# Attention and feed-forward kernel: the products with v moved from two steps of a pair into all five

## The chip, the cores and the metric

One NeuronCore of a Trainium2 chip. The metric is the device time of one execution in microseconds (us).

## The reference

```python
scores = q @ k.T / sqrt(D) + bias[h]        # per batch b, head h; bias from a small MLP on log distances
attn = exp(scores - max) / (sum + 1e-9)
out = attn @ v                              # B=4, H=8, S=576, D=64
x = out, heads side by side                 # 2304 x 512
h = x @ w_in                                # 512 x 2048
y = (h * tanh(softplus(h))) @ w_out         # 2304 x 512
```

All in float32.

## The kernel before

The program has three stages. The first makes the bias of all heads and writes it to DRAM (`make_h`, `mirrored`, `evac`). The second is attention, the loop over `step(n)`. The third is the feed-forward part in blocks of 512 or 256 tokens (`hidden`, `gate`, `project`).

The schedule is written by hand: each engine takes its instructions in the order in which the code calls them.

Attention goes by pairs: pair i is two heads of one batch, 16 pairs in all. The 576 query rows of a pair are cut into five chunks c: four of 128 rows for each of the two heads, and one (c = 4) with the last 64 rows of both heads in one tile. A pair has five steps, x = 0 to 4, that take the chunks in `ORDER = [0, 1, 4, 2, 3]`. So step x = 2 is the short one. What a step n does:

- `scores(n)` (L218) on TensorE: three passes of q @ k.T with high and low parts (L227), into one or two PSUM tiles `s` of a pool of two.
- `add_bias(n)` (L230) on VectorE: one instruction a head, adds the bias and finds the row extreme (L241). It frees the tile `s`.
- `exps` (L246) on ScalarE: exponentials with row sums (L256).
- `transposes(n - 2)` (L304): the chunk of two steps before is turned on TensorE in blocks of 128 keys (L296), and ScalarE copies the blocks into `main` (L313, L316). `main` and `tail` belong to a group: group 0 of a pair is chunks 0 and 1 (256 queries), group 1 is chunks 4, 2 and 3 (320 queries).
- `turn_tails` (L318), at x = 2 and x = 4: the last 64 keys of both heads of several chunks, and at x = 2 the reciprocals of the row sums (L325, L333, L337, L338), copied by ScalarE (L343).
- `products` (L345): o = v.T @ turned probabilities for one group, five blocks k of keys (the fifth is `tail`) for two heads, accumulated in one PSUM tile `o` of a pool of one (L352).
- `collect` (L355): VectorE copies `o` to `x` (L360), SP stores `x` to `x_d` (L362, L364, L365).
- `ahead` (L397): loads for later pairs: q and k (`load_hi` on POOL's queue, `load_raw` on SP's), `load_v`, and in every fourth pair the bias of the next heads.
- `split` (L422): VectorE makes the low part of the next pair's q and k, and converts a piece of the weights of the third stage (float64 to float32 by shifts and masks).

In the steady state `products(i - 1, 1)` stands at x = 2 before the transposes and `products(i, 0)` at x = 4 after them, each followed by its `collect` at the end of the same step.

Of the kernel before, what the change touches and what calls it, by code (L numbers as in the profile page):

```python
# [7 lines left out]
F32 = mybir.dt.float32  # L8
# [11 lines left out]
P = 128  # L20
# [24 lines left out]
def kernel(ctx: ExitStack, tc, qk, v, wb, w2, w_in, w_out, psia, psi4, rinv, eye, out):  # L45
    nc = tc.nc
    pe, dve, act, pool, sp = nc.tensor, nc.vector, nc.scalar, nc.gpsimd, nc.sync
# [46 lines left out]
    def load_weights():  # L94
        while todo and len(w64) < 2:
            kind, g, k = job = todo.pop(0)
            w = convp.tile([P, 512, 2], U32, name="w64")
            if kind == "i":
                src = w_in[k * P:(k + 1) * P, g * 512:(g + 1) * 512]
            else:  # L100
                src = w_out[(4 * g + k) * P:(4 * g + k + 1) * P, :]
            sp.dma_start(out=w.rearrange("p f t -> p (f t)"), in_=src.bitcast(U32))
            w64.append((job, w))
# [66 lines left out]
    def load_raw(i):  # L170
        hp, b = divmod(i, B)
        raw = rawp.tile([P, QW], F32, name="rawqk")
        if i < 2:
            dve.memset(raw[:, 0:1], 0.0)
        sp.dma_start(out=raw, in_=qk[b, hp])
        qk_raw[i] = raw

    def load_v(i):
        hp, b = divmod(i, B)
        vt = vp.tile([P, 2, 5, D], F32, name="vt")  # L180
        sp.dma_start(out=vt, in_=v[b, hp].rearrange("p (h c d) -> p h c d", h=2, c=5))
        v_t[i] = vt

    def load_hi(i):
        hp, b = divmod(i, B)
        hi = hip.tile([P, QW], F32R, name="qkhi", bufs=3)
        pool.dma_start(out=hi, in_=qk[b, hp])
        qk_hi[i] = hi
# [7 lines left out]
    def load_bias(hp, c):  # L196
        h0, h1 = 2 * hp, 2 * hp + 1
        rows = P if c < 4 else 64
        src = bias_d[c][:, :rows * PITCH].rearrange("h (i j) -> h i j", j=PITCH)[:, :, PAD:PAD + S]
        t = bias_t[hp, c] = biasp.tile([P, 2 * S if c < 4 else 640], F32, name=f"bias{c}")[:, :2 * S if c < 4 else S]  # L200
        if c < 4:
            sp.dma_start(out=t[:, 0:S], in_=src[h0])
            sp.dma_start(out=t[:, S + 64:], in_=src[h1, :, 0:512])
            sp.dma_start(out=t[:, S:S + 64], in_=src[h1, :, 512:S])
        else:
            for r in range(2):
                sp.dma_start(out=t[r * 64:r * 64 + 64], in_=src[h0 + r])

    NPAIR = B * HP
    steps = [(i, c) for i in range(NPAIR) for c in ORDER]  # L210
    steps[4:7] = [(1, ORDER[0]), (1, ORDER[1]), (0, ORDER[4])]
    NS = len(steps)
    pt_t, live, o_t, sums, rc = {}, {}, {}, {}, {}
# [16 lines left out]
    def add_bias(n):  # L230

        i, c = steps[n]
        bt = bias_t[i // B, c]
        m = st.tile([P, 2], F32, name="m")
        if c < 4:
            pt = pp.tile([P, 2 * S], F32, name="pt")
        else:
            pt = p4p.tile([P, 640], F32, name="pt4")[:, :S]
        for u, s in enumerate(live[n]):
            sl = slice(u * S, (u + 1) * S)  # L240
            dve.tensor_tensor_reduce(  # L241
                out=halves(pt[:, sl]), in0=s[:, :, :SH], in1=halves(bt[:, sl]),
                scale=-0.125, scalar=BIG, op0=ALU.add, op1=ALU.min, accum_out=m[:, u:u + 1])
        live[n] = (pt, m)

    def exps(n, u):  # L246

        i, c = steps[n]
        if u == 1 and c == 4:
            return  # L250
        if i not in sums:
            sums[i] = st.tile([P, 9], F32, name="sums", bufs=3)
        pt, m = live[n]
        ps = pt[:, u * S:(u + 1) * S]
        k = 4 * u + c if c < 4 else 8
        act.activation(ps, ps, AF.Exp, bias=m[:, u:u + 1], scale=-1.0, accum_out=sums[i][:, k:k + 1])  # L256
# [5 lines left out]
        dve.reciprocal(r, r)  # L262
        return r

    turned, pts = [], {}

    def store_reciprocals():
        i, turned_r = turned.pop()
# [17 lines left out]
    def x_tile():  # L286
        return xs.tile([P, 320], F32, name="x", bufs=2)
# [54 lines left out]
        for tail, off, c, w, rows in copies:  # L342
            act.copy(tail[rows, off:off + w], tp[rows, c:c + w])  # L343

    def products(i, grp):  # L345
        main, tail = pt_t.pop((i, grp))
        vt = v_t[i]
        w = 256 if grp == 0 else 320
        o_t[i, grp] = o = o_ps.tile([P, 512], F32, name="o")
        for k in range(5):  # L350
            for h in range(2):
                pe.matmul(o[h * 64:h * 64 + 64, :w], vt[:, h, k, :], main[:, h, k, :] if k < 4 else tail,  # L352
                          start=(k == 0), stop=(k == 4), skip_group_check=True)

    def collect():  # L355
        (i, grp), o = o_t.popitem()
        hp, b = divmod(i, B)
        w = 256 if grp == 0 else 320
        x = x_first.pop() if x_first else x_tile()
        dve.tensor_copy(x[:, :w], o[:, :w])  # L360
        if grp == 0:
            sp.dma_start(out=x_d[b][:, hp, 0:256], in_=x[:, :256])  # L362
        else:
            sp.dma_start(out=x_d[b][:, hp, 256:512], in_=x[:, 64:320])  # L364
            sp.dma_start(out=x_d[b][:, hp, 512:576], in_=x[:, 0:64])  # L365
# [7 lines left out]
    def load_x(blk, p):  # L373
        t0, n = blocks[blk]
        raw = p.tile([P, HP, TB], F32, name="xraw", bufs=1)
        for off, m, b, s in _x_runs(t0, n):
            sp.dma_start(out=raw[:, :, off:off + m], in_=x_d[b][:, :, s:s + m])
        x_raw[blk] = raw

    def load_r(blk, r, h0, h1):  # L380

        t0, n = blocks[blk]
        for off, m, b, s in _x_runs(t0, n):
            while m:
                k = min(m, 512 - s) if s < 512 else m
                for u in range(2):
                    if s < 512:
                        src = r_d[b][h0:h1, 4 * u:4 * u + 4].rearrange("p c j -> p (c j)")[:, s:s + k]
                    else:
                        src = r_d[b][h0:h1, 8, 64 * u + s - 512:64 * u + s - 512 + k]  # L390
                    sp.dma_start(out=r[64 * u:64 * u + 64, :, off:off + k],
                                 in_=src.unsqueeze(0).to_broadcast([64, h1 - h0, k]))
                off, m, s = off + k, m - k, s + k
# [3 lines left out]
    def ahead(n):  # L397

        i, x = divmod(n, 5)
        if n == 4:  # L400
            pool.tensor_copy(gate_t, live[n][1][:, 0:1])
        if x == (1 if i else 4) and i + 2 < NPAIR:
            load_hi(i + 2)
            load_raw(i + 2)
        if (n == 9 or x == 3 and i > 1) and i + 1 < NPAIR:
            load_v(i + 1)
        if n == 5:
            load_weights()
        if i % B == B - 1 and i // B + 1 < HP:
            load_bias(i // B + 1, ORDER[x])  # L410
        if n == NS - 11:
            load_x(0, x0)
        if n in (NS - 10, NS - 6):
            x_r[0] = x0.tile([P, 2, TB], F32, name="xr", bufs=1)
            h0 = 0 if n == NS - 10 else 2
            load_r(0, x_r[0], h0, h0 + 2)
        if n in (NS - 7, NS - 3):
            h0 = 0 if n == NS - 7 else 2
            for d in range(2):
                pool.tensor_tensor(x_raw[0][:, h0 + d], x_raw[0][:, h0 + d], x_r[0][:, d], op=ALU.mult)  # L420
# [14 lines left out]
    def step(n):  # L435
        i, x = divmod(n, 5)
        back = n - LAG

        def exponentials():
            if n < NS:  # L440
                exps(n, 0)
                exps(n, 1)

        if n < NS:
            scores(n)
            add_bias(n)
        if n == 9:
            products(0, 1)
        elif x == 2 and n > 7:
            turn_tails((i - 1, 2), (i - 1, 3))  # L450
            products(i - 1, 1)
            exponentials()
        for k in (0, 1) if n == 3 else (back,):
            if k < NS:
                transposes(k)
        if n == 5:
            turn_tails((0, 2))
        elif n == 8:
            turn_tails((0, 3), (1, 0), (1, 1))
        elif n == 9:  # L460
            turn_tails((1, 4))
        elif x == 4:
            turn_tails((i, 0), (i, 1), (i, 4))
        if x != 2 or n == 7:
            exponentials()
        if x == 4 and n != 9:
            products(i, 0)
        elif n == 8:
            products(1, 0)
        if n < NS:  # L470
            ahead(n)
        if n <= NS and steps[n - 1][1] == ORDER[4]:
            rc[steps[n - 1][0]] = reciprocals(steps[n - 1][0])
        if n < NS:
            split(n)
        if turned:
            store_reciprocals()
        if o_t:
            collect()


# [40 lines left out]
    for idx in range(NB + 2):  # L522
# [4 lines left out]
        if idx + 2 < NB:  # L527
            n = reach(ts[idx + 2])[2]
# [79 lines left out]
    o_ps = lpsum("o_ps", 1)  # L608
# [248 lines left out]
```

## Time and profile before

| | |
|---|---|
| median of 3 runs | 715.35 us (714.86 to 715.86) |
| the profiled execution | 714.97 us |
| its span, first to last instruction | 713.0 us |
| TensorE busy (PE) | 670.4 us, 94% |
| VectorE busy (DVE) | 518.3 us, 73% |
| ScalarE busy (ACT) | 461.2 us, 65% |

PE is TensorE's matmuls, PEld its weight loads, DVE VectorE, ACT ScalarE, POOL GpSimd, SP SyncE. Idle time before an instruction is put down to what released it. Matmul rows overlap, because they are pipelined; where the argument needs what one costs, it goes by the starts of neighbouring rows. In the trace a float32 matmul of the products is two instructions, so x20 there is ten matmuls.

### The profile page before, as it was taken

How to read it: one execution, taken by the hardware profiler on the slowest of the kernel's cores; microseconds unless marked ns; L12 is line 12 of the kernel's file. 1: busy time of each engine (PE TensorE's matmuls, PEld its weight loads, DVE VectorE, ACT ScalarE, POOL GpSimd, SP SyncE). 2: the span in 40 equal slices, each digit the busy share in tenths (PEclk: the TensorE clock that was granted, in tenths of full speed). 3: DMA queues.
4: the chain of work that ended last, by engine and by line, in shares of the span. 5: the costliest groups of instructions: out<-in, count | busy, mean ns of one | idle time of the engine just before them, and what ended most of it. 6: DMA issues, size and time to landing. Idle time of an engine off the chain costs nothing.

```text
span 713.0 us, 14055 instructions
## 1 busy us (share of the span) xinstructions
PE 670.4 (94%) x5456; PEld 520.2 (73%) x5456; DVE 518.3 (73%) x1053; ACT 461.2 (65%) x949; POOL 17.9 (3%) x27
## 2 busy tenths in 40 slices
PE   6988989988999898898999999999999999999997
PEld 3546666666667666666878888889988888888886
DVE  7896677777887777558888888875675666665564
ACT  6987788878888888745565656553645454444443
POOL 0000000000000002100000000000000000000000
PEclk9999999999999999999999999999999999999999
DMA  8888677558647755050123312304141000010001
GB/s 278 271 272 288 225 236 248 171 171 282 196 169 222 255 177 155 27 158 29 60 88 105 103 59 60 112 7 119 60 112 36 1 1 0 1 59 1 1 0 60
DMA packets 46435, 86.94 MB, mean 122 GB/s; under 512 B 13200, under 2 KB 22048, under 8 KB 46368
## 3 DMA queue, kind: packets, MB, share of 16 engines
q1 hardware_dynamic: 43488, 75.32, 33.5%
q0 software_dynamic: 2304, 10.49, 4.6%
q8 instruction: 43, 0.70, 0.4%
q10 hardware_dynamic: 576, 0.22, 0.1%
q14 instruction: 24, 0.20, 0.1%
HBM read 64.56 MB, written 21.45 MB: 121 GB/s over the span
## 4 chain that ended last, share of the span: by engine, by line
PE 76%; DVE 14%; ACT 4%; DMA 2%; issue 2%; SPq 1%; DVEq 0%; ACTq 0%
PE y L702 24%; PE h L657 24%; PE o L352 11%; PE s L227 9%; DVE pt L241 6%; PE bps L557 5%; PE tp L296 2%; PE tp L325 1%; DVE e L680 1%; DVE e L664 1%; DVE w L134 1%; ACT bt L563 1%; DVE e L679 1%; DMA bias<-bias_d 1%; DVE w L127 1%
## 5 line engine op out<-in xcount | busy, mean ns | idle before, releaser
L241 DVE CUSTOM_DVE_ANT_0 pt<-s,bias 128x576 f32<-128x576 f32 x144 | 103.8, 754 | 38.0 <-PE s L227 35.1
L702 PE MATMUL y<-who,ghi 128*128 128x512 f32 x288 | 112.5, 391 | 2.5 <-ACT ghi L681 1.6
L702 PE MATMUL y<-who,glo 128*128 128x512 f32 x288 | 112.4, 390 | 1.3 <-DVE glo L684 1.3
L681 ACT CAST ghi<-e 128x512 fp32r<-128x512 f32 x72 | 44.7, 621 | 105.5 <-DVE e L680 99.4
L256 ACT ACTIVATE pt<-pt,m 128x576 f32<-128x576 f32 x144 | 111.5, 782 | 1.5 <-DVE m L241 1.1
L702 PE MATMUL y<-wlo,ghi 128*128 128x512 f32 x288 | 112.2, 390 | 0.0
L313 ACT COPY main<-tp 128x512 f32<-128x512 f32 x126 | 67.9, 592 | 37.3 <-PE tp L296 36.5
L657 PE MATMUL h<-xhi,whi 128*128 128x512 f32 (+1 forms) x320 | 80.0, 372 | 1.7 <-ACT xhi L632 1.7
L684 DVE TENSOR_TENSOR glo<-e,ghi 128x512 fp32r<-128x512 f32 x72 | 49.7, 691 | 42.0 <-ACT ghi L681 42.0
L657 PE MATMUL h<-xhi,wli 128*128 128x512 f32 (+1 forms) x320 | 79.5, 371 | 0.0
L657 PE MATMUL h<-xlo,whi 128*128 128x512 f32 (+1 forms) x320 | 78.8, 368 | 0.0
L227 PE MATMUL s<-qkhi 64*128 64x288 f32 (+1 forms) x288 | 54.4, 353 | 22.3 <-DVE m L241 22.2
L662 ACT ACTIVATE e<-h 128x512 f32<-128x512 f32 x72 | 42.7, 593 | 45.7 <-PE h L657 45.7
L663 DVE TENSOR_SCALAR e<-e 128x512 f32<-128x512 f32 x72 | 30.6, 425 | 55.7 <-ACT e L662 55.7
L352 PE MATMUL o<-main,vt 128*64 128x320 f32 (+1 forms) x512 | 69.1, 412 | 0.9 <-ACT main L313 0.9
L657 PEld LDWEIGHTS h<-xhi,whi 128*128 128x128 f32 x320 | 57.6, 189 | 13.5 <-ACT xhi L632 2.6
L657 PEld LDWEIGHTS h<-xhi,wli 128*128 128x128 f32 x320 | 57.5, 190 | 10.1
L702 PEld LDWEIGHTS y<-who,ghi 128*128 128x128 f32 x288 | 54.1, 188 | 14.5 <-ACT ghi L681 2.5
L657 PEld LDWEIGHTS h<-xlo,whi 128*128 128x128 f32 x320 | 57.1, 189 | 10.1
L702 PEld LDWEIGHTS y<-who,glo 128*128 128x128 f32 x288 | 54.1, 188 | 14.2 <-DVE glo L684 2.9
L702 PEld LDWEIGHTS y<-wlo,ghi 128*128 128x128 f32 x288 | 54.1, 188 | 10.8
L227 PEld LDWEIGHTS s<-qkhi 64*128 64x128 f32 (+1 forms) x288 | 29.6, 186 | 41.4 <-DVE m L241 35.0
(71 smaller groups left out, 1048.6 us busy)
## 6 DMA issues: line engine op xcount, KB each, us to landing
bias_d<-bt SPq DMA_DIRECT2D x36, 295.5 KB
qkhi<-in_qk_dram POOLq DMA_DIRECT2D x16, 640.0 KB, 4.7
rawqk<-in_qk_dram SPq DMA_DIRECT2D x16, 640.0 KB
w<-in_w_in_dram SPq DMA_DIRECT2D x16, 512.0 KB
w<-in_w_out_dram SPq DMA_DIRECT2D x16, 512.0 KB
vt<-in_v_dram SPq DMA_DIRECT2D x16, 320.0 KB
bias<-bias_d SPq DMA_DIRECT2D x16, 288.0 KB
out_dram<-w SPq DMA_DIRECT2D x17, 256.0 KB
```

Of the source, the lines that this page charges most:

```text
L227: pe.matmul(live[n][h][:, j, :SH], stat[rows, c * P:(c + 1) * P], mov[rows, k0:k0 + SH], start=(k == 0), stop=(k == 2))
L241: dve.tensor_tensor_reduce(out=halves(pt[:, sl]), in0=s[:, :, :SH], in1=halves(bt[:, sl]), scale=-0.125, scalar=BIG, op0=ALU.add, op1=ALU. ...
L256: act.activation(ps, ps, AF.Exp, bias=m[:, u:u + 1], scale=-1.0, accum_out=sums[i][:, k:k + 1])
L313: (dve.tensor_copy if n < 2 and u else act.copy)(blocks[:, :, off + 64 * u:off + 64 * u + 64], tp)
L352: pe.matmul(o[h * 64:h * 64 + 64, :w], vt[:, h, k, :], main[:, h, k, :] if k < 4 else tail, start=(k == 0), stop=(k == 4), skip_group_chec ...
L557: pe.matmul(ps[cg * 32:cg * 32 + 32, a:b], w2t, src, start=True, stop=True)
L657: pe.matmul(h[:, u * n:(u + 1) * n], w["i", g4, d][:, r * P:(r + 1) * P], x[:, d, :n], start=(k == 0), stop=(k == 11))
L662: act.activation(e, h, AF.Exp)
L663: dve.tensor_scalar(e, e, E20, None, op0=ALU.min)
L681: act.copy(ghi, e)
L684: dve.tensor_tensor(glo, e, ghi.bitcast(F32), op=ALU.subtract)
L702: pe.matmul(ys[blk][t], g[:, c0:c0 + P], w, start=((blk, f) in first and k == 0), stop=((blk, f) in last and k == 2))
```

## The change

`products` takes a range of blocks k, and from the third pair on (n > 11) the ten matmuls of a group are called in several steps. Group 1 of the pair before: blocks 0 and 1 at x = 2, blocks 2 to 4 at x = 3. Group 0: block 0 at x = 4, blocks 1 and 2 at x = 0 of the next pair, 3 and 4 at x = 1. `collect` follows the step with block 4. `load_v` moves from x = 3 to x = 4, since v of the pair before is now read at x = 3. The calls of `turn_tails` are the same ones as before. The last blocks of the last pair follow in `step(80)` to `step(82)`.

```diff
--- before.py
+++ after.py
@@ -262,7 +262,7 @@
         dve.reciprocal(r, r)
         return r
 
-    turned, pts = [], {}
+    turned, done, pts = [], [], {}
 
     def store_reciprocals():
         i, turned_r = turned.pop()
@@ -342,18 +342,23 @@
         for tail, off, c, w, rows in copies:
             act.copy(tail[rows, off:off + w], tp[rows, c:c + w])
 
-    def products(i, grp):
-        main, tail = pt_t.pop((i, grp))
+    def products(i, grp, ks=range(5)):
+        main, tail = pt_t[i, grp]
         vt = v_t[i]
         w = 256 if grp == 0 else 320
-        o_t[i, grp] = o = o_ps.tile([P, 512], F32, name="o")
-        for k in range(5):
+        if 0 in ks:
+            o_t[0] = o_ps.tile([P, 512], F32, name="o")
+        for k in ks:
             for h in range(2):
-                pe.matmul(o[h * 64:h * 64 + 64, :w], vt[:, h, k, :], main[:, h, k, :] if k < 4 else tail,
+                pe.matmul(o_t[0][h * 64:h * 64 + 64, :w], vt[:, h, k, :], main[:, h, k, :] if k < 4 else tail,
                           start=(k == 0), stop=(k == 4), skip_group_check=True)
+        if 4 in ks:
+            del pt_t[i, grp]
+            done.append((i, grp))
 
     def collect():
-        (i, grp), o = o_t.popitem()
+        i, grp = done.pop()
+        o = o_t[0]
         hp, b = divmod(i, B)
         w = 256 if grp == 0 else 320
         x = x_first.pop() if x_first else x_tile()
@@ -402,7 +407,7 @@
         if x == (1 if i else 4) and i + 2 < NPAIR:
             load_hi(i + 2)
             load_raw(i + 2)
-        if (n == 9 or x == 3 and i > 1) and i + 1 < NPAIR:
+        if x == 4 and 0 < i < NPAIR - 1:
             load_v(i + 1)
         if n == 5:
             load_weights()
@@ -448,7 +453,7 @@
             products(0, 1)
         elif x == 2 and n > 7:
             turn_tails((i - 1, 2), (i - 1, 3))
-            products(i - 1, 1)
+            products(i - 1, 1, range(2 if n < NS else 5))
             exponentials()
         for k in (0, 1) if n == 3 else (back,):
             if k < NS:
@@ -463,10 +468,13 @@
             turn_tails((i, 0), (i, 1), (i, 4))
         if x != 2 or n == 7:
             exponentials()
-        if x == 4 and n != 9:
-            products(i, 0)
-        elif n == 8:
-            products(1, 0)
+        if n in (4, 8):
+            products(n // 8, 0)
+        elif n > 11:
+            if x == 3:
+                products(i - 1, 1, range(2, 5))
+            elif x != 2:
+                products(i if x == 4 else i - 1, 0, {4: (0,), 0: (1, 2), 1: (3, 4)}[x])
         if n < NS:
             ahead(n)
         if n <= NS and steps[n - 1][1] == ORDER[4]:
@@ -475,7 +483,7 @@
             split(n)
         if turned:
             store_reciprocals()
-        if o_t:
+        if done:
             collect()
```

TensorE in the steady state, from the tails of x = 2 to the transposes of x = 3, before (s are scores, tp blocks being turned, o products with v):

```order
L325 MATMUL tp<-ident,pt 128x128 x2
L333 MATMUL tp<-ident,sums 9x128
L352 MATMUL o<-main_3555,vt 64x320 x8
L352 MATMUL o<-tail_3556,vt 64x320 x2
L296 MATMUL tp<-ident,pt 128x64 x16
L227 MATMUL s<-qkhi 128x288 x4
L227 MATMUL s<-qklo,qkhi 128x288 x4
L227 MATMUL s<-qkhi,qklo 128x288 x4
L296 MATMUL tp<-ident,pt 128x64 x16
```

The same steps in the changed kernel:

```order
L325 MATMUL tp<-ident,pt 128x128 x2
L333 MATMUL tp<-ident,sums 9x128
L353 MATMUL o<-main_3812,vt 64x320 x4
L296 MATMUL tp<-ident,pt 128x64 x16
L227 MATMUL s<-qkhi 128x288 x4
L227 MATMUL s<-qklo,qkhi 128x288 x4
L227 MATMUL s<-qkhi,qklo 128x288 x4
L296 MATMUL tp<-ident,pt 128x64 x16
L353 MATMUL o<-main_3812,vt 64x320 x4
L353 MATMUL o<-tail_3813,vt 64x320 x2
```

The products of 320 columns, one run of ten matmuls before, are two pieces now: four before the transposes of x = 2, and six after those of x = 3.

TensorE from the tails of x = 4 on, before:

```order
L325 MATMUL tp<-ident,pt 128x128 x2
L337 MATMUL tp<-ident,pt_3697 64x128
L338 MATMUL tp<-ident,pt_3697 128x128
L352 MATMUL o<-main_3716,vt 64x256 x8
L352 MATMUL o<-tail_3717,vt 64x256 x2
L227 MATMUL s<-qkhi 128x288 x4
L227 MATMUL s<-qklo,qkhi 128x288 x4
L227 MATMUL s<-qkhi,qklo 128x288 x4
L296 MATMUL tp<-ident,pt 128x64 x16
L227 MATMUL s<-qkhi 128x288 x4
```

The same places in the changed kernel, up to the last products of the group in x = 1:

```order
L353 MATMUL o<-main_3710,vt 64x256 x2
L227 MATMUL s<-qkhi 128x288 x4
L227 MATMUL s<-qklo,qkhi 128x288 x4
L227 MATMUL s<-qkhi,qklo 128x288 x4
L296 MATMUL tp<-ident,pt 128x64 x16
L353 MATMUL o<-main_3710,vt 64x256 x4
L227 MATMUL s<-qkhi 128x288 x4
L227 MATMUL s<-qklo,qkhi 128x288 x4
L227 MATMUL s<-qkhi,qklo 128x288 x4
L296 MATMUL tp<-ident,pt 128x64 x16
L353 MATMUL o<-main_3710,vt 64x256 x2
L353 MATMUL o<-tail_3711,vt 64x256 x2
```

The products of 256 columns were ten matmuls in a row; now two stand after the tails, four after the transposes of x = 0 and four after those of x = 1.

VectorE from the end of x = 2 on, before (ISA is the bias add and the read of its result):

```order
L120 TENSOR_SCALAR low<-w_3851 128x512
L271 COPY rt<-tp 9x128
L360 COPY x<-o 128x320
L241 ISA pt,m<-s,bias_4063 128x576
L241 ISA m 128x1
L241 ISA pt,m<-s,bias_4063 128x576
L241 ISA m 128x1
L127 SCALAR_TENSOR_TENSOR w_4331<-high,low 128x512
```

And in the changed kernel:

```order
L120 TENSOR_SCALAR low<-w_3843 128x512
L271 COPY rt<-tp 9x128
L241 ISA pt,m<-s,bias_4057 128x576
L241 ISA m 128x1
L241 ISA pt,m<-s,bias_4057 128x576
L241 ISA m 128x1
L127 SCALAR_TENSOR_TENSOR w_4325<-high,low 128x512
L365 COPY x<-o 128x320
```

The copy x<-o of the group of 320 columns has moved from the end of x = 2 to the end of x = 3, behind two bias adds and a conversion.

## Rows read from the trace of the kernel before

**Rows 1.** Busy by stretch: length, PE, PEld, DVE, ACT, POOL; clock, DMA share, GB/s

```profile
84.80:290.89 206.09, 186.54 (x2251) 137.12 (x2253) 159.68 (x387) 173.04 (x438) 12.09 (x15) 1.00 0.64 202
```

**Rows 2.** Timeline of PE (start, us, ...): such products, first and 14th

```profile
84.80 1.57 PE L352 MATMUL o<-main,vt 128*64 128x320 f32 x10 [0.20 <-ACT main L313]
...
290.83 2.37 PE L352 MATMUL o<-main,vt 128*64 128x320 f32 x16
```

**Rows 3.** Waits, 84.80 to 290.89 us: us in total, times, longest

```profile
ACT main L313 <- PE tp L296: 32.6, 33, 1.7
...
DVE pt L241 <- PE s L227: 25.2, 38, 1.0
PE s L227 <- DVE m L241: 19.2, 65, 0.4
...
PEld tp L296 <- issue: 6.4, 13, 0.5
```

**Rows 4.** Timeline of PE in one pair, from x = 2

```profile
178.18 0.53 PE L227 MATMUL s<-qkhi 128*128 128x288 f32 x2 [0.24 <-DVE m L241]
...
179.08 0.38 PE L325 MATMUL tp<-ident,pt 128*128 128x128 f32 x2
...
179.52 2.37 PE L352 MATMUL o<-main,vt 128*64 128x320 f32 x16
...
182.36 0.71 PE L296 MATMUL tp<-ident,pt 64*128 64x64 f32 x16
182.89 0.51 PE L227 MATMUL s<-qkhi 64*128 64x288 f32 x4
...
183.77 0.75 PE L296 MATMUL tp<-ident,pt 64*128 64x64 f32 x16
...
186.23 0.54 PE L296 MATMUL tp<-ident,pt 64*128 64x64 f32 x8
186.69 0.44 PE L325 MATMUL tp<-ident,pt 128*128 128x128 f32 x2
186.97 0.27 PE L337 MATMUL tp<-ident,pt 128*64 128x128 f32 x1
187.08 0.27 PE L338 MATMUL tp<-ident,pt 128*128 128x128 f32 x1
187.28 1.95 PE L352 MATMUL o<-main,vt 128*64 128x256 f32 x16
189.06 0.60 PE L352 MATMUL o<-tail,vt 128*64 128x256 f32 x4
189.59 0.54 PE L227 MATMUL s<-qkhi 64*128 64x288 f32 x4
...
190.49 0.66 PE L296 MATMUL tp<-ident,pt 64*128 64x64 f32 x16
```

**Rows 5.** Timeline of DVE in the same pair

```profile
182.48 0.49 DVE L360 COPY x<-o 128x320 f32<-128x320 f32 x1
183.96 0.76 DVE L241 CUSTOM_DVE_ANT_0 pt<-s,bias 128x576 f32<-128x576 f32 x1 [0.99 <-PE s L227]
...
186.43 0.76 DVE L241 CUSTOM_DVE_ANT_0 pt<-s,bias 128x576 f32<-128x576 f32 x1 [0.42 <-PE s L227]
...
190.69 0.76 DVE L241 CUSTOM_DVE_ANT_0 pt<-s,bias 128x576 f32<-128x576 f32 x1 [0.56 <-PE s L227]
...
193.27 0.75 DVE L241 CUSTOM_DVE_ANT_0 pt<-s,bias 128x576 f32<-128x576 f32 x1
```

**Rows 6.** Timeline of ACT in the same pair

```profile
183.17 0.59 ACT L313 COPY main<-tp 128x512 f32<-128x512 f32 x1 [1.16 <-PE tp L296]
```

**Rows 7.** Busy in a pair that loads bias, columns as rows 1

```profile
227.00:242.77 15.77, 14.35 (x176) 10.54 (x175) 11.96 (x30) 13.54 (x36) 0.53 (x1) 1.00 0.94 307
```

**Rows 8.** Timeline where attention meets the third stage

```profile
301.64 1.07 ACT L313 COPY main<-tp 128x512 f32<-128x512 f32 x2 [0.48 <-PE tp L296]
...
303.28 1.31 PE L657 MATMUL h<-xhi,whi 128*128 128x512 f32 x2 [1.68 <-ACT xhi L632]
```

## The prediction

> **What bounds the kernel now.** I read the busy times by stage first, then the waits of the middle stage, then TensorE's timeline through one pair, then VectorE's through the same pair.
>
> The change touches only the attention loop. From 84.80 us to 290.89 us there are 13 repetitions of one pair: the products of a second group start at 84.80 us, and 13 pairs later at 290.83 [rows 2], 206.03 / 13 = 15.85 us each. No engine fills it: ScalarE is busy 173.04 / 13 = 13.31 us of a pair, VectorE 12.28, TensorE 14.35 by its busy rows [rows 1]. In the waits [rows 3] three engines wait for one another: ScalarE's copies of turned blocks for the transposes (32.6 us, 2.5 a pair), VectorE's bias adds for the scores, the scores for the bias adds.
>
> The timeline says why [rows 4]. Of the five steps of a pair (x = 0 to 4) two carry all products: x = 2 from 179.52 to 182.36, x = 4 from 187.28 to 189.59. In those TensorE is late and VectorE waits 0.99 and 0.56 us for scores [rows 5]. In the other three TensorE has scores and transposes only, some 1.4 us, and is held by the two score buffers: scores may start when the bias adds of the step before have read theirs. That loop, bias add to bias add, takes 186.43 - 183.96 = 2.47 us [rows 5]. So a pair is two steps bound by TensorE and three by the loop.
>
> **TensorE's own work in a pair**, from start to start of neighbouring rows [rows 4], since busy rows overlap. Scores: 0.90 (x = 2), 0.88 (x = 3), 0.90 (x = 0); 0.89 taken for x = 1 and 4, whose rows hold waits; 4.46 in all. Transposes: 0.53 for 16 (182.36 to 182.89), four times, and 0.46 for x = 4: 2.58. Tails: 0.44 (179.08 to 179.52) and 0.59 (186.69 to 187.28): 1.03. Products: 2.84 + 2.31 = 5.15. Sum 13.22; so 15.85 - 13.22 = 2.63 us a pair are waits.
>
> The Trainium skill (Perfetto Trace Analysis, Identifying the Most-Contended Engine) says that matmul busy time is no good measure of TensorE's headroom, because the instructions are pipelined. Here by the busy rows there would be 15.85 - 14.35 = 1.50 us a pair to win, less 0.54 for the new edges below: 13 x 0.96 = 12.5 us, an end at 702.5 us. The starts give more room and bear the page out.
>
> **What the change adds and moves.**
> - *Products.* Nothing is removed; ten matmuls of each group stay, but one block k (two matmuls) goes to x = 4, two to x = 0, two to x = 1 (256 columns, 1.78 / 8 = 0.22 us a matmul), and for 320 columns two blocks to x = 2 and three to x = 3 (0.275 us a matmul, (2.84 - 0.09) / 10).
> - *New edges.* Products use other shapes of the array (128*64) than their neighbours (64*128, 128*128). Two groups become five, so three more entries and three more exits. In the rows an exit costs 189.59 - 189.06 - 2 x 0.22 = 0.09 us, and an entry 187.28 - 187.08 = 0.20 against 0.11 between the transposes before it, again 0.09. Six by 0.09 is 0.54 us a pair. The dearest reading is the idle time of the weight load behind the products of x = 2, 6.4 us / 13 = 0.49 [rows 3]; I take 0.09, since a load that waits behind a running matmul delays nothing until that ends. The Trainium skill (TensorEngine Tiling (Array Packing), Key Properties) states that changing the tiling mode, not just the tile, drains TensorE, which speaks against this change; it gives no time. The 0.09 agrees that an edge costs something; by a drain as long as that idle time the sum would turn (third rival).
> - *Steps after*, scores + transposes + tails + products + edges: x = 2: 0.90 + 0.53 + 0.44 + 1.10 + 0.09 = 3.06. x = 3: 0.88 + 0.53 + 1.65 + 0.18 = 3.24. x = 4: 0.89 + 0.46 + 0.59 + 0.44 + 0.09 = 2.47. x = 0: 0.90 + 0.53 + 0.89 + 0.18 = 2.50. x = 1: 2.49. Sum 13.76. None is below the loop's 2.47, so TensorE should no longer wait for it by much; three steps stand level with it.
> - *VectorE.* The copy of o (0.49 us [rows 5]) moves to the end of x = 3 and x = 1. It waits for the last product, and the bias adds queue behind it; but those need the next scores, 0.88 to 0.90 us on TensorE, which cover the copy. o has one bank: the next group's first product waits for the copy, and has scores and tails before it, 0.90 + 0.44 = 1.34 us at x = 2 and 0.89 + 0.46 + 0.59 = 1.94 at x = 4. Cost nothing; without that cover up to 0.49 each.
> - *A level step costs something.* x = 0 has the reciprocals and a conversion on VectorE ahead of the next bias add: 193.27 - 190.69 = 2.58 us [rows 5], 0.11 over the loop. I take 0.11 for each of the three level steps and 0.11 for hand-overs to ScalarE: 0.44. Bounds: 0, if all is covered, and 0.9, if ScalarE (13.31 us of work) becomes what is late and keeps 1.35 us of its waits (second case below). Period 13.76 + 0.44 = **14.2 us**.
> - *Transposes at x = 2* come 1.65 us earlier (six products of 0.275 no longer stand before them), which takes away ScalarE's wait there, 1.16 us [rows 6].
> - *Queues.* On SP the load of v moves one step later (x = 3 to 4), used a whole pair later; the stores of x move behind raw and weight loads, the reciprocals' store stays. POOL's order does not change. Cost nothing: the cover is five steps, some 14 us. The gather of the first x block now follows its last store by a step; POOL's multiply after it has several steps left. Pairs that load the next bias move 307 GB/s at a DMA share of 0.94 [rows 7]; at full share that is 327, or 14.8 us for the same bytes, 0.6 over the new period in three pairs: 0 to 1.8 us, taken as 0, since the mean over all pairs is 202 GB/s [rows 1] and the bias tiles have a whole pair to land.
> - *The end.* The last pair's first group moves out of x = 4: two blocks fall into the 1.68 us that TensorE waits for ScalarE's casts [rows 8], two behind the first hidden product. The casts follow a copy that waited 0.48 us for transposes, which is won; the late blocks and their copy give about 0.5 back. Taken as 0.
>
> **Sum.** 13 x (15.85 - 14.2) = 21.5 us. The profiled execution took 714.97 us (span 713.0 and 1.97 around it), 0.38 below the median of the runs. 714.97 - 21.5 = **693.5 us**.
>
> **Rivals.**
> 1. *All cover holds*: 13.76 a pair, 13 x 2.09 = 27.2, 687.8 us. Against: three steps level with the loop, ScalarE at 97%.
> 2. *ScalarE becomes the bound.* Its copies wait for transposes and its exponentials for bias adds, in one hand-written order. Of its 2.51 us of waits a pair, the 1.16 at x = 2 [rows 6] go; if the rest stays, the period is 13.31 + 1.35 = 14.66: 13 x 1.19 = 15.5, 699.5 us. For: a pair that loads bias has 13.54 us of work [rows 7]. Against: the rest are waits for TensorE in steps that were starved.
> 3. *Slower: the edges drain.* If an edge costs nearly what the weight load idles behind products, taken as 0.43 of the 0.49, six cost 2.58, the period is 13.22 + 2.58 + 0.44 = 16.24, 13 x 0.39 = 5.1 longer: 720.1 us. It decides from (15.85 - 0.44 - 13.22) / 6 = 0.365 us an edge. Against: matmul starts show 0.09 at both kinds of edges. (The page on tiling named above would stand behind this case.)
> 4. *No change: the bank of o.* The copy comes late at both hand-overs, about 0.8 us each, and takes back the 1.65: 715. For: VectorE's order has two bias adds and a conversion before the copy at x = 3. Against: the bias adds, 1.44 us with what follows them, run while six products (1.65 us) do.
> That the products do not spread is excluded: TensorE's order shows five pieces.
>
> **How the numbers follow.** Forecast 62%, the first rival 12%, the second 18%, the third 4%, the fourth 4%. The range takes in the first rival's 687.8 and the second's 699.5 with the three bias pairs' 1.8: 687 to 702, and leaves out the last two rivals and the rest of such mixtures. A measurement tells 0.2%, 1.4 us, from no change. Faster 0.92 (the first three cases), same 0.04, slower 0.04.
>
> **What would show it.** A period near 14.2 us between the products of second groups; VectorE's waits for scores and the scores' waits for bias adds both far below now's; the copies' wait for transposes well under 2.5 us a pair; exit and entry at 0.09 us; ScalarE's busy share at 93% or more. Wrong would be: a score row waiting for bias adds by 0.3 us in every step as now, product rows that wait for the copy of o, gaps of 0.4 us at product edges, or a period over 15.

## The result and the profile after

The changed kernel takes 692.6 us (median of 4 runs, 690.43 to 692.85) against 715.61 us before: ratio 0.9673, 95% interval 0.9652 to 0.9694. The forecast was 693.5 us. The profiled execution took 692.42 us with a span of 690.5, against 714.97 and 713.0.

The first and the 14th start of products of a second group in the timeline of TensorE, changed kernel (start us, us, engine), which answer to [rows 2]:

```profile
85.56 1.30 PE L353 MATMUL o<-main,vt 128*64 128x320 f32 x8 [0.18 <-ACT main L313]
...
269.12 1.30 PE L353 MATMUL o<-main,vt 128*64 128x320 f32 x8
```

13 pairs take 183.56 us, 14.12 each, where they took 206.03 and 15.85. That is 22.47 of the 22.5 us by which the span fell. Ahead of them the kernel is 0.76 us later, behind them 422.17 - 421.38 = 0.79 us shorter: the rest of the program takes as long as before within 0.8 us.

Busy times of that stretch, columns as in [rows 1]:

```profile
85.56:269.12 183.56, 183.18 (x2250) 132.04 (x2250) 157.55 (x387) 174.12 (x438) 8.75 (x14) 1.00 0.70 226
```

The work has not changed: ScalarE 174.12 us against 173.04, VectorE 157.55 against 159.68. TensorE's rows now cover all but 0.38 us of the stretch. ScalarE is busy 95% of it.

The waits of that stretch (us in total, times, longest), which answer to [rows 3]:

```profile
DVE pt L241 <- PE s L227: 18.8, 40, 1.0
...
PEld tp L296 <- issue: 6.4, 13, 0.5
...
ACT main L316 <- PE tp L296: 4.7, 10, 0.5
...
ACT main L313 <- PE tp L296: 3.8, 11, 0.5
...
PEld s L227 <- DVE m L241: 2.3, 6, 0.4
```

ScalarE's wait for transposes fell from 32.6 us to 8.5: 3.8 in the copies of the four long chunks (L313) and 4.7 in those of the short chunk (L316), which had no such wait before. The scores' wait for bias adds, 19.2 us on TensorE itself before, is gone from its matmul rows; on the weight loads of the scores 2.3 us are left under this name, where there were 30.1. VectorE's wait for scores fell only from 25.2 to 18.8 us.

One pair of TensorE's timeline, from the scores of x = 2 to the products of the next x = 2, which answers to [rows 4]:

```profile
183.20 0.53 PE L227 MATMUL s<-qkhi 128*128 128x288 f32 x2
...
184.31 0.27 PE L333 MATMUL tp<-ident,sums 128*9 128x128 f32 x1
184.51 1.30 PE L353 MATMUL o<-main,vt 128*64 128x320 f32 x8
185.74 0.72 PE L296 MATMUL tp<-ident,pt 64*128 64x64 f32 x16
186.26 0.52 PE L227 MATMUL s<-qkhi 64*128 64x288 f32 x4
...
187.18 0.84 PE L296 MATMUL tp<-ident,pt 64*128 64x64 f32 x16
187.95 1.30 PE L353 MATMUL o<-main,vt 128*64 128x320 f32 x8
...
189.71 0.53 PE L227 MATMUL s<-qkhi 64*128 64x288 f32 x4
...
191.53 0.65 PE L353 MATMUL o<-main,vt 128*64 128x256 f32 x4
192.11 0.72 PE L227 MATMUL s<-qkhi 64*128 64x288 f32 x4
...
193.06 0.21 PE L296 MATMUL tp<-ident,pt 64*128 64x64 f32 x1
...
193.78 1.08 PE L353 MATMUL o<-main,vt 128*64 128x256 f32 x8
194.80 0.53 PE L227 MATMUL s<-qkhi 64*128 64x288 f32 x4
...
195.69 0.65 PE L296 MATMUL tp<-ident,pt 64*128 64x64 f32 x16
196.28 0.65 PE L353 MATMUL o<-main,vt 128*64 128x256 f32 x4
196.76 0.60 PE L353 MATMUL o<-tail,vt 128*64 128x256 f32 x4
197.29 0.53 PE L227 MATMUL s<-qkhi 128*128 128x288 f32 x2
...
198.60 1.30 PE L353 MATMUL o<-main,vt 128*64 128x320 f32 x8
```

From score start to score start the steps take: x = 2 3.06 us, x = 3 3.45, x = 4 2.40, x = 0 2.69, x = 1 2.49; the forecast had 3.06, 3.24, 2.47, 2.50, 2.49. No score row in this pair has a wait in front of it; the first at x = 0 is long (192.11, 0.72 us where the others have 0.52 or 0.53). A wait is hidden in that row. The scores of the two heads go side by side: at x = 1 the first matmuls of both start at 194.80. At x = 0 the first matmul of one head starts at 192.11, that of the other only at 192.30, as this cut of TensorE's timeline shows (the matmuls that run at 192.51), together with the instruction of VectorE that reads the result of the last bias add of x = 4:

```profile
192.30 0.40 PE L227 MATMUL s<-qkhi 64*128 64x288 f32 x2
...
192.16 0.08 DVE L241 DVE_READ_ACCUMULATOR2_ANT m<- 128x1 f32 x1
```

So the second head's scores start 0.06 us after that read ends, and 0.19 us after the first head's: the wait for the second score buffer is still there at x = 0.

VectorE's timeline in the same pair:

```profile
186.98 0.27 DVE L271 COPY rt<-tp 9x128 f32<-9x128 f32 x1
187.33 0.76 DVE L241 CUSTOM_DVE_ANT_0 pt<-s,bias 128x576 f32<-128x576 f32 x1
...
190.80 0.76 DVE L241 CUSTOM_DVE_ANT_0 pt<-s,bias 128x576 f32<-128x576 f32 x1 [0.48 <-PE s L227]
...
193.27 0.76 DVE L241 CUSTOM_DVE_ANT_0 pt<-s,bias 128x576 f32<-128x576 f32 x1
```

Two things are seen there. The copy `rt` of x = 2 ends at 187.25, when the transposes of x = 3 are due (they start at 187.18, 0.92 us after their scores, and take 0.77 up to the products). And from x = 4 to x = 0 the bias adds stand exactly 193.27 - 190.80 = 2.47 us apart, the loop of [rows 5].

### The profile page after: what moved, and what is told of

It is laid out like the page before. It is cut to its first block, busy times and chain, and to the rows that moved or that the text cites. A ratio compares the mean times of both kernels' runs of the same rounds, so it can differ in the third digit from the quotient of the medians.

```text
span 690.5 us, 14085 instructions
## 1 busy us (share of the span) xinstructions
PE 668.3 (97%) x5456; PEld 515.7 (75%) x5456; DVE 516.3 (75%) x1053; ACT 462.2 (67%) x949; POOL 16.6 (2%) x27
## 4 chain that ended last, share of the span: by engine, by line
PE 84%; DVE 7%; ACT 6%; issue 1%; DMA 1%; DVEq 0%; ACTq 0%
PE y L710 25%; PE h L665 25%; PE o L353 12%; PE s L227 10%; PE tp L296 5%; PE bps L565 4%; ACT pt L256 2%; PE tp L325 1%; ACT main L313 1%; DVE e L688 1%; DVE e L672 1%; ACT bt L571 1%; DVE e L687 1%; DVE w L127 1%; DVE w L134 1%
## 5 line engine op out<-in xcount | busy, mean ns | idle before, releaser
L353 PE MATMUL o<-main,vt 128*64 128x320 f32 (+1 forms) x512 | 78.4, 420 | 0.6 <-ACT main L313 0.2
L313 ACT COPY main<-tp 128x512 f32<-128x512 f32 x126 | 67.8, 593 | 7.5 <-PE tp L296 6.2
L710 PEld LDWEIGHTS y<-who,ghi 128*128 128x128 f32 x288 | 54.1, 188 | 14.2 <-ACT ghi L689 2.2
L296 PEld LDWEIGHTS tp<-ident,pt 64*128 64x128 f32 x1152 | 49.5, 138 | 10.8 <-issue 7.4
L688 DVE TENSOR_TENSOR e<-e,r 128x512 f32<-128x512 f32 x72 | 49.9, 693 | 7.9 <-DVE e L687 0.5
```

What stands on the lines that cost most here:

```text
L296: pe.transpose(tp[:, k * 64:(k + 1) * 64], pt[rows, c0:c0 + P], ident[rows, rows])
L313: (dve.tensor_copy if n < 2 and u else act.copy)(blocks[:, :, off + 64 * u:off + 64 * u + 64], tp)
L353: pe.matmul(o_t[0][h * 64:h * 64 + 64, :w], vt[:, h, k, :], main[:, h, k, :] if k < 4 else tail, start=(k == 0), stop=(k == 4), skip_group ...
L688: dve.tensor_tensor(e, e, r, op=ALU.mult)
L710: pe.matmul(ys[blk][t], g[:, c0:c0 + P], w, start=((blk, f) in first and k == 0), stop=((blk, f) in last and k == 2))
```

## The experiments

Theory: the gain is TensorE work put into the steps in which it waited for the two score buffers, place by place. Rivals: it comes from the transposes of x = 2, which reach ScalarE earlier; it comes from the load of v; only TensorE's total counts; edges of products are dear.

Outside the pairs two executions can differ by more than a microsecond. The kernel with the copy of the reciprocals first (below) was profiled twice. From the 14th products of a second group to the end it took 419.88 us in one execution and 421.08 in the other. TensorE waited 1.81 us for ScalarE's casts there in both. Then its granted clock fell to half, the lower of its two levels (1.2 GHz), for 3.4 us in the second, and stayed at the full 2.4 GHz in the first (columns as in [rows 1], the clock third from the end):

```profile
279.80:283.20 3.40, 3.36 (x15) 2.08 (x17) 1.88 (x4) 0.97 (x3) 0.00 (x0) 1.00 0.93 281
...
280.80:284.20 3.40, 3.40 (x8) 2.42 (x9) 1.90 (x4) 0.92 (x2) 0.00 (x0) 0.50 0.83 270
```

The profiled executions of the kernel before and of the changed kernel both have this fall. Differences of 1 to 2 us between other kernels are therefore read from the 13 pairs as well, from the first to the 14th start of products of a second group: 206.03 us before, 183.56 in the changed kernel.

**One half of the change at a time.** First group 1 alone is spread, group 0 stays whole (the cut is against the changed kernel, as are the others unless said):

```diff
             if x == 3:
                 products(i - 1, 1, range(2, 5))
-            elif x != 2:
-                products(i if x == 4 else i - 1, 0, {4: (0,), 0: (1, 2), 1: (3, 4)}[x])
+            elif x == 4:
+                products(i, 0)
```

> Group 1 (320 columns) spread over x = 2 and x = 3 as in the change, group 0 in one run at x = 4 as before. Theory (the gain is TensorE work put into steps in which it waited for the two score buffers, place by place): steps of before from effective score start to score start are x=2 4.71, x=3 2.57, x=4 4.13, x=0 2.60, x=1 1.79, together 15.80 us; only x=2 and x=3 change, to 3.06 and 3.45 as measured in the changed kernel, x=4 stays near 4.2: period about 15.1 to 15.2, 706 to 707 us. Rival (the earlier transposes of x=2 relieve ScalarE and that makes the gain): nearly the whole gain stays, 693 to 696 us.

Measured 706.67 us, ratio 0.9887 (0.9870 to 0.9904): 8.7 us less than the 715.33 of the kernel before, measured beside it. TensorE's timeline of this kernel from x = 4 to x = 2:

```profile
185.88 0.53 PE L227 MATMUL s<-qkhi 64*128 64x288 f32 x4
...
188.47 0.53 PE L227 MATMUL s<-qkhi 64*128 64x288 f32 x3 [0.28 <-DVE m L241]
...
190.36 0.53 PE L227 MATMUL s<-qkhi 128*128 128x288 f32 x2 [0.34 <-DVE m L241]
```

x = 0 and x = 1, which got no products, wait as before: 2.59 and 1.89 us, counted from the rows that waited.

Then group 0 alone, group 1 in one run at x = 2:

```diff
-            products(i - 1, 1, range(2 if n < NS else 5))
+            products(i - 1, 1)
...
-            if x == 3:
-                products(i - 1, 1, range(2, 5))
-            elif x != 2:
+            if x not in (2, 3):
                 products(i if x == 4 else i - 1, 0, {4: (0,), 0: (1, 2), 1: (3, 4)}[x])
```

> Group 0 (256 columns) spread over x = 4, 0 and 1 as in the change, group 1 in one run at x = 2 as before. Theory: x=2 and x=3 stay 4.71 and 2.57, x=4, 0, 1 become 2.40, 2.69, 2.49 as in the changed kernel: period 14.86, 13 x 0.95 = 12 us less than before, 703 us. Both halves of the change together then give the whole (9 + 12 against 22). Rival (ScalarE's wait at x=2 makes the gain): that wait stays, no gain to speak of, 713 to 716 us.

Measured 701.32 us, ratio 0.9813 (0.9796 to 0.9830): 14.0 less. The halves give 8.7 + 14.0 = 22.7 us, the whole 23.0. In the 13 pairs the halves take 197.80 and 193.80 us, which is 8.2 and 12.2 less than before, 20.4 together of the whole's 22.5. So most of the gain adds up place by place; of the 14.0, 12.2 is in the pairs, as expected, and the rest lies outside them. What the halves lack is in waits of their own: with group 1 alone x = 3 takes 3.45 to 3.76 us, and with group 0 alone the first product of group 1 stands 0.45 us later in three pairs of 13 and 0.83 in a fourth, waiting for the copy of o.

**Earlier transposes, nothing spread.** The kernel before with the run of products behind the transposes of x = 2:

```diff
             turn_tails((i - 1, 2), (i - 1, 3))
-            products(i - 1, 1)
             exponentials()
...
+        if x == 2 and n > 7:
+            products(i - 1, 1)
         if x == 4 and n != 9:
             products(i, 0)
```

> The kernel before, but at x = 2 the whole run of products stands behind the transposes and no longer ahead of them, so that ScalarE gets its blocks 2.8 us earlier; nothing is spread. Theory: TensorE's work and the starved steps are the same, 715 us within 1.5. Rival (ScalarE's wait of 1.16 us at x = 2 is what the change removes): 13 x 1.16 = 15 us less, 700 us.

Measured 716.91 us, ratio 1.0025 (1.0015 to 1.0036), 1.6 us more. Waits of this kernel in its pairs:

```profile
ACT main L313 <- PE tp L296: 33.5, 26, 2.2
...
PE s L227 <- DVE m L241: 19.9, 64, 0.4
```

ScalarE waits as long as before (32.6 us), only elsewhere (in one pair 1.61 us ahead of the copies of x = 3), and the scores wait as before (19.2). The rival falls: the earlier transposes alone give nothing. That ScalarE's wait is a result of TensorE's starved steps fits this and its fall in the changed kernel.

**The load of v alone**, in the kernel before:

```diff
-        if (n == 9 or x == 3 and i > 1) and i + 1 < NPAIR:
+        if x == 4 and 0 < i < NPAIR - 1:
             load_v(i + 1)
```

> The kernel before with the load of v one step later, at x = 4, as in the change, and nothing else. Theory: nobody waits for it, 715.4 us within 1. Rival (the place of the load on SP's queue is a part of the gain): 5 us or more less.

Measured 716.19 us, ratio 1.0005 (0.9992 to 1.0017), with 205.98 us for the 13 pairs against 206.03. It gives nothing.

**One more edge.** In the changed kernel block 1 goes ahead of the transposes of x = 0:

```diff
+        if n > 11 and x == 0:
+            products(i - 1, 0, (1,))
         for k in (0, 1) if n == 3 else (back,):
...
-                products(i if x == 4 else i - 1, 0, {4: (0,), 0: (1, 2), 1: (3, 4)}[x])
+                products(i if x == 4 else i - 1, 0, {4: (0,), 0: (2,), 1: (3, 4)}[x])
```

> The changed kernel, but at x = 0 block 1 stands before the transposes and block 2 behind them: one more entry and one more exit of products a pair, no other work. Theory (TensorE is the bound now, each edge costs about 0.09 us, an entry behind transposes up to 0.15): 0.18 to 0.3 us a pair, 2.3 to 3.9 us in 13 pairs: 695 to 696.5 us. Rival (a drain near 0.43 us an edge): 0.86 a pair, 704 us. Rival (x = 0 is held by VectorE's loop and has room): 692.6 us.

Measured 696.27 us, ratio 0.9743 (0.9727 to 0.9758), 3.7 above the changed kernel's 692.6. TensorE's timeline at x = 0 and the start of x = 1:

```profile
194.25 0.72 PE L227 MATMUL s<-qkhi 64*128 64x288 f32 x4
...
195.42 0.65 PE L353 MATMUL o<-main,vt 128*64 128x256 f32 x4
196.00 0.71 PE L296 MATMUL tp<-ident,pt 64*128 64x64 f32 x16
196.65 0.65 PE L353 MATMUL o<-main,vt 128*64 128x256 f32 x4
197.23 0.53 PE L227 MATMUL s<-qkhi 64*128 64x288 f32 x4
```

The step takes 2.98 us instead of 2.69: 0.29 for two edges, 0.145 each on average, or 13 x 0.29 = 3.8 us, near the 3.7 of the medians. The 13 pairs of the profiled execution are 188.31 - 183.56 = 4.75 us longer; the rest is at x = 2 and x = 3 of some pairs. So work added to TensorE at x = 0 is paid in full, and an edge is far below the 0.365 us from which the change would have been a loss.

**Block 0 taken out of x = 4** and put to x = 0:

```diff
-            elif x != 2:
-                products(i if x == 4 else i - 1, 0, {4: (0,), 0: (1, 2), 1: (3, 4)}[x])
+            elif x < 2:
+                products(i - 1, 0, {0: (0, 1, 2), 1: (3, 4)}[x])
```

> The changed kernel, but block 0 of group 0 goes from x = 4 to x = 0, to blocks 1 and 2: four pieces, two edges fewer, x = 4 without products. Theory (a step that is below the loop of scores and bias adds waits for it): x = 4 has 1.9 us of work on TensorE and still takes about 2.5, x = 0 grows by 0.44: period up by about 0.4 to 0.5, 13 pairs by 5 to 6.5: 698 to 699 us. Rival (only TensorE's total counts): two edges less, 13 x 0.18 = 2.3 us faster, 690 us.

Measured 697.51 us, ratio 0.9751 (0.9738 to 0.9765), 4.9 above the changed kernel. TensorE's timeline from x = 4 to x = 1:

```profile
192.21 0.53 PE L227 MATMUL s<-qkhi 64*128 64x288 f32 x4
...
194.79 0.53 PE L227 MATMUL s<-qkhi 64*128 64x288 f32 x3 [0.28 <-DVE m L241]
...
197.72 0.54 PE L227 MATMUL s<-qkhi 64*128 64x288 f32 x4
```

Counted in the same way, x = 4 has less work and takes 2.58 us instead of 2.40, with the old wait back, and x = 0 grows to 2.93. Two edges less did not help: the total is not all that counts.

**The copy of the reciprocals first** at x = 2, in the changed kernel:

```diff
+        if turned:
+            store_reciprocals()
         if n < NS:
             split(n)
-        if turned:
-            store_reciprocals()
```

> The changed kernel, but VectorE copies the turned reciprocals (rt) before it splits q and k at x = 2, and no longer after that split and a conversion. In the changed kernel the transposes of x = 3 start about when that copy ends, since it holds one of three banks; x = 3 took 3.45 us where the starts of its parts give 3.24. Theory: that copy is what x = 3 waits for; the step falls by 0.1 to 0.2 us, 13 pairs by 1.3 to 2.6: 690 to 691.5 us. Rival (the 0.21 are dearer edges of the products): no change, 692.6 us.

Measured 690.21 us, ratio 0.9662 (0.9642 to 0.9682). In one pair of it the scores of x = 3 and those of x = 4 start 3.32 us apart instead of 3.45:

```profile
185.83 0.52 PE L227 MATMUL s<-qkhi 64*128 64x288 f32 x4
...
189.15 0.53 PE L227 MATMUL s<-qkhi 64*128 64x288 f32 x4
```

VectorE pays with a wait, in total 8.5 us in its pairs:

```profile
DVE rt L271 <- ACT tail L343: 8.5, 13, 1.4
```

The copy and ScalarE's copy of the tails read the same PSUM tile, and in this kernel the one waits for the other. So it was tried between the split of q and k and the conversion as well, together with the changed kernel and a second time the copy first:

```diff
             split_qk(i + 1)
+        if turned:
+            store_reciprocals()
         if w32:
             lower_weights(dve)
```

> The changed kernel itself, beside the next three on one chip: 692 to 693 us.

> The kernel with the copy of the reciprocals first at x = 2, again. If the earlier 690.2 against 692.6 us is real: 1.5 to 2.5 us below the changed kernel of the same call. If it was the chip: the same.

> The changed kernel with the copy of the reciprocals between the split of q and k and the conversion. The copy then ends at about 186.75 in the changed kernel's pair, before the transposes of x = 3 can start (187.14), and VectorE does not wait for ScalarE's copy of the tails as it does when the copy comes first (8.5 us in 13 pairs). TensorE is the bound: the same as with the copy first, 690 us; if VectorE's wait there cost something too: 688 to 689 us.

Measured side by side: 691.89 us (0.9675, 0.9661 to 0.9689) for the change, 690.39 (0.9658, 0.9643 to 0.9672) with the copy first, 690.37 (0.9650, 0.9637 to 0.9663) with it in between. That is 1.5 us less in either place, at the edge of what the intervals tell apart. The 13 pairs take 183.58 us with the change, 182.70 with the copy first and 182.54 with it in between: 0.9 and 1.0 us less. That part is in the pairs, where x = 3 takes 3.33 to 3.35 us in 12 of the 13 with the earlier copy, and 3.45 in nine of the 13 of the changed kernel; the rest of the 1.5 us lies outside them. These are the fastest versions tried.

**Group 1 whole at x = 3**, with the copy first:

```diff
-            products(i - 1, 1, range(2 if n < NS else 5))
+            products(i - 1, 1, range(0 if n < NS else 5))
...
             if x == 3:
-                products(i - 1, 1, range(2, 5))
+                products(i - 1, 1)
```

> The changed kernel with the copy of the reciprocals first, and group 1 in one run at x = 3, none of it at x = 2: four pieces, two edges fewer. x = 2 then has 1.8 us of TensorE's work, without a loop behind it since its bias add is one instruction. If TensorE's total is all that counts: 0.18 to 0.3 us a pair less than with the copy first alone, 687 to 689 us. Rival: VectorE has 3 us in x = 2 (bias add, split of q and k, conversion) and the scores of x = 3 and their bias adds queue behind it, but x = 3 is now 4.4 us long and covers that: same. Second rival: the transposes of x = 3 come before ScalarE has freed the banks (its exponentials of x = 1 and x = 2 stand before its copies), 0.5 to 1 us a pair more: 697 to 704 us.

Measured 702.11 us, ratio 0.9822 (0.9799 to 0.9844), 11.9 above the version with the copy first. TensorE's timeline at x = 3:

```profile
192.08 0.27 PE L296 MATMUL tp<-ident,pt 64*128 64x64 f32 x1
193.01 0.71 PE L296 MATMUL tp<-ident,pt 64*128 64x64 f32 x15 [0.66 <-ACT main L313]
```

The second transposes stand 0.93 us behind the first, waiting for ScalarE to free a bank, in ten of the first 13 pairs, and 0.65 in the others. That is most of the loss, and the second rival of that run holds.

**Nothing at x = 1**, on the version with the copy in between:

```diff
-            elif x != 2:
-                products(i if x == 4 else i - 1, 0, {4: (0,), 0: (1, 2), 1: (3, 4)}[x])
+            elif x in (0, 4):
+                products(i if x == 4 else i - 1, 0, {4: (0, 1), 0: (2, 3, 4)}[x])
```

> As the run before, but group 0 in two pieces: blocks 0 and 1 at x = 4, 2 to 4 at x = 0, none at x = 1; two edges fewer. In the kernel before, x = 1 took 1.79 us from score start to score start, not 2.47, because the scores of x = 2 need one buffer only. Theory (x = 1 has a floor of 1.8 us): its 1.42 us of work on TensorE leave 0.37 of waits, the two edges give back 0.25 and the wait at x = 4 to x = 0 some 0.1: the same as the run before within 1.5 us. Rival (x = 1 is level with the loop of 2.47 us as the forecast had it): 0.7 us a pair more, 9 us longer, 699 us.

Measured 691.22 us, ratio 0.9662 (0.9649 to 0.9675): 0.85 us above the version with products there, where the rival had 9. In the 13 pairs it takes 184.42 us against 182.54, 1.9 more, and its profiled execution has no fall of the clock behind them. So it is close to the same, a little slower if anything. TensorE's timeline at x = 1:

```profile
195.40 0.53 PE L227 MATMUL s<-qkhi 64*128 64x288 f32 x4
...
197.32 0.53 PE L227 MATMUL s<-qkhi 128*128 128x288 f32 x2 [0.36 <-DVE m L241]
```

x = 1 takes 1.92 us, not 2.47. Its floor is lower: the scores of x = 2 fill one buffer, so they need only the first of the two bias adds of x = 1, for which they wait 0.36 us.

## Why the prediction was right

*Two steps bound by TensorE, three by the loop.* Shown: each half of the change wins back the waits of its own steps and leaves the others (the two half kernels), and emptying x = 4 brings its wait back.

*13.22 us of TensorE's own work, by starts and not by busy rows.* The room was there: the pair fell by 1.73 us, more than the 1.50 that busy rows left. The sentence of the Trainium skill on matmul busy time (Perfetto Trace Analysis, Identifying the Most-Contended Engine) agrees with these rows.

*Edges at 0.09 us.* Right for entries, somewhat low for exits. At x = 1 of the changed kernel the last transposes start at 196.12 and the products at 196.28, 0.15 us later, where transposes follow one another by 0.06: 0.09 for the entry, and it is the same at x = 0. Exits cost 185.74 - 184.51 - 4 x 0.275 = 0.13 and 192.11 - 191.53 - 2 x 0.2225 = 0.135 us. The direct test gives 0.145 each. The drain that the Trainium skill states (TensorEngine Tiling (Array Packing), Key Properties) has this size at most here; the 0.43 of the third rival is excluded.

*The level steps, 0.44 us.* The period came out at 14.12 us instead of 14.2, so the term was 0.36, but it did not lie where the forecast put it. x = 1 took just its work (2.49), and it was never level with a loop of 2.47: the last run shows 1.92 when it is empty. x = 4 took 0.07 less than its sum. The excess lies in x = 0 (2.69 against 2.50) and x = 3 (3.45 against 3.24). At x = 0 it is the 0.19 us that the second head's scores wait for the last bias add of x = 4, the loop of 2.47 us; from 192.30 on the step takes 2.50, as in the sum. At x = 3 the transposes are due as the `rt` copy ends; with that copy earlier the step takes 3.33, so it makes 0.12 of the 0.21, and what makes the other 0.09 is open. The forecast had not followed that copy: in its paragraph on VectorE it moved the copy of o and left out `rt`, which holds one of the three banks of the transposes. So that the total came near 0.44 is in part luck.

*Hand-over of o.* Nearly right: it costs 0.4 us in all, not nothing. Behind x = 4 the bank is free in time. Behind x = 1 the first product of the next group waits for the copy of o in three of the 13 pairs, those in which VectorE's conversion ahead of the copy is the longest. The list of waits does not name it. One of them:

```profile
226.59 0.27 PE L333 MATMUL tp<-ident,sums 128*9 128x128 f32 x1
226.95 1.30 PE L353 MATMUL o<-main,vt 128*64 128x320 f32 x8
...
226.38 0.42 DVE L365 COPY x<-o 128x256 f32<-128x256 f32 x1
```

The products start 0.35 us behind the last of the tails, where 0.20 is usual (184.31 to 184.51), and 0.15 behind the end of the copy, as in the other two pairs. That is the fourth rival's mechanism, but 0.15 us in three pairs instead of about 0.8 at both hand-overs of every pair.

*VectorE's waits for scores* were to fall far below the 25.2 us of before, and fell to 18.8 only. In the pair shown VectorE still waits 0.48 us for the scores of x = 4. That sign did not come; VectorE waits because TensorE, whose rows now cover the stretch, brings the scores late.

*ScalarE*: not the bound, its copies into `main` wait (3.8 + 4.7) / 13 = 0.65 us a pair. *Queues*: the move of the load of v costs nothing. The pair that loads bias, after, and the next one:

```profile
212.70:226.95 14.25, 14.17 (x175) 10.18 (x174) 12.23 (x31) 13.74 (x36) 0.53 (x1) 1.00 0.95 319
226.95:240.92 13.97, 13.97 (x173) 10.16 (x173) 11.95 (x31) 12.98 (x34) 0.53 (x1) 1.00 0.66 225
```

It takes 0.28 us more than the next, at 319 GB/s; before, with its 15.77 us [rows 7], it was below the mean pair. The 0.28 is no cost of the DMA: the late start at 226.95 is one of the three waits for the copy of o, and it ends the one stretch and begins the other. From the scores of one x = 2 to those of the next the pair takes 14.09 us and the one behind it 14.13.

*The end* came to -0.79 us, taken as 0. TensorE waits for the casts there still:

```profile
280.13 2.35 PE L665 MATMUL h<-xhi,whi 128*128 128x512 f32 x4 [1.81 <-ACT xhi L640]
```

The 1.81 us stand against 1.68 [rows 8], although two blocks were moved in front of them: ScalarE sets that end.

## What to carry to other kernels

Where steps of one kind are starved by a ring of two engines and two buffers, and others are too long, look for each step's floor and move accumulating matmuls into the starved ones until they reach it; beyond the floor every piece costs its full time, and below it the wait returns. Count a matmul engine's work by starts of rows, and price the cut itself (0.09 to 0.15 us at each edge here) from a place where it already occurs. A wait that ends on another engine may be an effect of the same starvation: moving that one thing alone, as in the kernel with the transposes first, tells whether it makes the gain. And a row without a wait in front of it can still hold one: look at the starts of single matmuls where a row is longer than its like.

## What the runs showed that was not expected

An edge between products and their neighbours costs 0.145 us when added at x = 0, against 0.09 read from the longer runs of before. And the same 16 transposes with the entry behind them take 196.28 - 195.69 = 0.59 us at x = 1 of the changed kernel, but 193.78 - 193.06 = 0.72 at x = 0. The wait that is hidden in the scores of x = 0 makes that difference: the late head's last scores start at 193.06, 0.13 us behind the other head's and together with the first transpose, and in both steps the products start 0.15 us behind the last transpose.
